# A fused attention, MoE and routed-expert kernel: expert 0's rows gathered before the last tile is stored, and a routing round in fewer instructions

## The chip, the cores and the metric

One core of a Trainium2 chip. The metric is the device time of one execution in microseconds (us), the median of several runs.

Engine names: PE or TensorE does matmuls, PEld is its load of stationary weights, DVE is VectorE, ACT is ScalarE, POOL is GpSimd (it also issues the indirect DMAs), SP is SyncE, which here only issues DMAs.

## What is computed

Three steps, cut to what matters here:

```python
# 1. retention-style attention: x is 3072 tokens x 512
# 2. a dense block
h = x @ w_in;  g = h * np.tanh(softplus(h));  x2 = g @ w_out          # 512 -> 2048 -> 512
# 3. a routed block: 8 experts, each takes exactly 3072 / 8 = 384 tokens
flat = (x2 @ w_gate).flatten()
for idx in np.argsort(-flat):                 # best (token, expert) pairs first
    tok, e = idx // 8, idx % 8
    if assigned[tok] < 0 and counts[e] < 384:
        assigned[tok] = e;  counts[e] += 1
for e in range(8):
    out[assigned == e] = relu(x2[assigned == e] @ w1[e]) @ w2[e]
```

Matrix products are done on pairs of 16-bit halves, three matmuls for one product.

## The kernel before

**Stages.** Tokens go in 8 groups of 384 (`G`), each of 3 tiles of 128 (`C`). For each group the attention, then `h_phase` (the first half of the dense block) and `x_phase` (the second half, a tile at a time: 48 matmuls of 512 columns into one PSUM bank, a square on ScalarE for the scale, a split into two 16-bit halves `xr`, and a DMA of these rows to `xbuf` in DRAM). When the logits of all groups are there, the routing starts while the last seven tiles of `x_phase` still run: three of group 6, three of group 7, and one tile of group 5 that was kept back ("late", its columns reloaded from `gbuf`). Then come the experts 0 to 7, one after the other.

**Routing** (`route_round`, lines 691 to 792) has eight rounds. A round finds which expert fills up next and which tokens it takes: each token's best logit `M` becomes an integer key, its five digits are compared one after the other with all thresholds (`against`, line 686, on VectorE), 24 matmuls count the tokens above each threshold (`pc`, line 729), one matmul spreads the answer (`pn`, line 734), and VectorE goes on to the next digit. At the end two matmuls (`pp`, lines 776 and 777) give each token its place in the expert's list, and the taken tokens' logits in `L` are set to a very low number. `route_list` (line 796) then turns places into a list of row numbers, `IDX[r]`, by 24 matmuls `pl` (line 819).

**An expert's data.** `weights(i)` (line 847; i is 0 for w1, 1 for w2) loads an expert's matrix into a half of `RAW` by an indirect DMA from GpSimd's queue (line 862), squares it on ScalarE in four parts (line 868), and splits it in four parts into `WIN` (even experts) or `WOUT` (odd ones), ScalarE and VectorE each doing one half (lines 228 and 229). `prep_x(r)` (line 885) gathers the expert's 384 rows from `xbuf` by three indirect DMAs (line 890) and turns them: for expert 0 by 24 transposes on TensorE (line 902) and three copies out of PSUM on VectorE (line 903), for the others by a DMA that transposes. `expert(r)` (line 907) has a first half of 8 times 12 matmuls, evicted by lines 918 to 920, and a second half of 3 times 24, evicted by line 936 and scattered to the output by line 937.

**What sets the order.** `Weave` (line 43) is a planner: a main generator yields the cost of what it has just issued, side generators yield a wait after which they are due, and when the planner's clock passes a due time that side issues its next piece. The numbers in `KN` are such waits (`rw`: before a round's counts, `rs`: a correction for each step of each round, `lw`: before a list's matmuls, `fw` and `fs`: the weights' waits). From line 1124 on the instructions of TensorE, and from line 1145 on those of ScalarE, stay in the order in which they were issued; on VectorE, GpSimd and SyncE the order is left to the scheduler of the framework, by priority and readiness. The end of the program, from line 1140:

```python
    wv.add(logits(NG - 1), KN['st'][0]);  wv.add(routing(), KN['st'][1])
    wv.add(lists(), 21.0, 0);  wv.add(weights(0), KN['st'][2], 0);  wv.add(weights(1), KN['st'][3], 0)
    wv.run(x_phase(NG - 2))
    ...
    wv.run(x_phase(NG - 1))
    wv.run(x_phase(NG - 3, late, GB[0]))
    XD.append(1)
    wv.add(tokens())                       # calls prep_x(r) as soon as IDX[r] is known
    for r in range(E):
        need(lambda: r in XTE and r in SPL)
        wv.run(expert(r))
```

Of the kernel before, what the change touches and what calls it, by code (L numbers as in the profile page):

```python
# [39 lines left out]
KN = dict(ea=1, sc=1, pw=4, le=0.0, hl=['P', 'P'], cs=['V', 'V', 'V', 'V', 'V', 'V', 'V'], cc=['V', 'V', 'V', 'V', 'V', 'V', 'V', 'V', 'V'], lo=['c0', 'g', 'c1', 'm', 'c2', 's', 'wg', 'w0', 'w1', 'w2'], ga=['', 'V'], rs=[[-0.63, 0.3, -1.2, 0.0, 0.24, 0.0, 0.09, 0.0, 0.21, 0.0, 0.0, -4.24], [2.1, 0.09, 2.19, 0.0, 0.58, 0.15, 0.18, 0.15, 0.26, 0.26, 1.46, -0.41], [3.26, 0.0, -0.68, 0.2, 0.33, 0.0, -0.3, 0.0, 0.09, -0.12, 0.3, -3.18], [0.56, 0.0, 0.38, 0.0, 0.15, 0.0, 0.12, -0.11, -0.04, -0.27, 0.03, -3.34], [0.67, 0.0, 0.31, -0.76, 0.89, 0.0, 0.15, -0.22, 0.0, 0.0, -0.16, -4.15], [1.46, -2.35, 0.04, -0.29, 0.13, -2.18, 0.42, -0.4, 0.45, 0.03, 1.16, -4.07], [0.45, 0.54, 0.45, 0.0, 1.18, 0.0, -0.39, -0.55, -0.61, -0.05, 0.45, -3.57], [-0.15, 0.0, -0.75, 0.0, 0.0, 0.0, 0.0, -0.3, 0.0, 0.0, 3.28, -3.01]], fs=[[0.0, 0.0, -3.96, -1.22], [-0.75, 0.0, 1.32, 0.16], [0.0, 0.0, -2.08, 0.13], [0.0, -1.13, 0.71, 0.36], [0.0, 0.0, 0.0, -0.56], [0.38, 0.75, 0.13, 0.04], [0.0, 0.38, 0.2, 0.69], [0.0, -1.5, -0.61, 0.29]], av=[5.75, 5.75, 2.0, 4.0], a2=[1.3, 2.2, 4.3], a1=[0.1, 1.0, 0.85], ao=[3.5, 3.5, 3.35], wv=[8.5, 0.5, 1.0, 4.5], ov=5.0, an=[3.0, 3.15, 3.6], qm=['P0', 'VP', 'VP', 'PH', 'P1', 'VV', 'VP'], vm=['P0', 'VP', 'VP', 'VP', 'VP', 'P0', 'VP'], km=['A', 'H', 0, 0, 0, 0, 0], am=['AP', 'AP', 'AP', 'AV', 'AP', 'AV', 'VP'], ss=['V', 'P', 'P', 'P', 'P', 'P', 'P'], sm=['P', 'V', 'V', 'P', 'E', 'D', 'P'], ym=[0, 0, 0], hm=['VVVP', 'VVAV', 'VVVP', 'VVVP', 'AVVP', 'VVVP', 'VVVP', 'VVVP', 'VVVP'], ci=['AP'] * 8, co=['AP'] * 8, wa=[15, 12, 8, -1, 7, 16], cp=[0, 100, 0, 100], np=0, yp=[0, 2000], op=[0, 0, 200, 0, 50, 1000], xp=[0, 0, 0, 0, 0, 0], ld=[0, 1, 2, 3, 4], wj=[4, 4, 4], fw=[13.5, 18.5, 14, 16, 14, 16], qs=1.0, tw=3.0, sw=1.5, po=[[0] * 8] * 4, sl=[0, 0, 0.7], rw=[4.9, 2.5, 1.55, 1.7, 1.7], pn=0.5, lw=14.0, gx=9.0, tk=2.75, st=[16.0, 21.0, 20.0, 23.5], wi=['H', 'A', 0, 0, 2, 0, 0, 0], wo=['H', 'H', 0, 0, 0, 0, 'H', 0], tp=[], gw=5.15, nw=1.0, cw=0, sp=50, ap=1000, wp=None, ip=None)  # L40
# [58 lines left out]
def moe_kernel(ctx, tc, qkv, w_in, w_out, w_gate, w1p, w2p,  # L99
# [32 lines left out]
    V.tensor_scalar(identf, jp, 0.0, None, op0=OP.is_equal)  # L132
    tri = cst.tile([128, 128], BF, name="tri")
    V.tensor_scalar(tri, jp, 0.0, None, op0=OP.is_gt)
# [471 lines left out]
    def x_phase(g, cs=range(CPG), gb=None):  # L606
# [3 lines left out]
        for c in cs:  # L610
# [11 lines left out]
            SY.dma_start(xbuf[r:r + C, :], xr)  # L622
            yield PC[0] * 0.216


    RT, IDX, EWI, EWF = {}, {}, {}, []

    def route_setup():
# [62 lines left out]
    def route_round(r):  # L691
# [150 lines left out]
    def ps_any():  # L842
        return next(banks)()
# [370 lines left out]
```

## Time and profile before

| | us |
|---|---|
| median of 3 runs | 1097.4 (1096.71 to 1100.52) |
| the profiled execution | 1102.12 |
| span of the profile, first to last instruction | 1100.2 |
| TensorE busy | 965.7 |
| VectorE busy | 766.8 |
| ScalarE busy | 664.3 |
| GpSimd busy | 404.3 |

The profile is one execution, 4.7 us above the median. Times inside it are counted from the first instruction. A "view" is an answer that the trace gives: waits by engine, a chain of work followed back from the end, a list of instructions in order of time, or a table by stretch. In a row of the timeline `[1.14 <-DVE se0a L192]` says that the engine sat idle for 1.14 us and that VectorE's line 192 ended that. A row with `x12` is a run of 12 instructions merged; the busy time of a run of matmuls includes the drain of the last one.

### The profile page before, as it was taken

The numbers are of one execution on the slowest core, as the hardware profiler recorded it, in microseconds if no ns is written. First come the engines' busy times: TensorE is split into PE (matmuls) and PEld (weight loads), VectorE is DVE, ScalarE is ACT, GpSimd is POOL, SyncE is SP. The second block draws the span as 40 slices with busy tenths as digits, with TensorE's granted clock in tenths as the row PEclk, the third lists the DMA queues.
The fourth block names the chain that finished last, engine by engine and source line by source line (L and its number), as shares of the span: only waits on it lengthen the run. The fifth ranks groups of instructions, "written<-read, shape, count | busy, mean of one in ns | idle before, by whom it ended". The sixth has DMA issues, their size and how long they took to land.

```text
span 1100.2 us, 19751 instructions
## 1 busy us (share of the span) xinstructions
PE 965.7 (88%) x7897; PEld 558.3 (51%) x7897; DVE 766.8 (70%) x1742; ACT 664.3 (60%) x1010; POOL 404.3 (37%) x289
## 2 busy tenths in 40 slices
PE   3358768878999999999999989999599998989997
PEld 2345544444665555655556546545355554545553
DVE  6799979752666777677786755567778896795430
ACT  6457887742467577577567667415357676567741
POOL 4745553650542653543555423300312402304111
PEclk9959988878999999999999999999699999999999
DMA  9551361148113113122134110032555644728400
GB/s 316 173 156 42 106 192 38 39 91 167 27 53 86 41 49 87 39 64 62 49 87 83 45 39 1 10 117 114 159 177 164 179 148 153 233 84 263 140 29 29
DMA packets 108812, 113.65 MB, mean 103 GB/s; under 512 B 92464, under 2 KB 92592, under 8 KB 106672
## 3 DMA queue, kind: packets, MB, share of 16 engines
q1 hardware_dynamic: 102576, 66.24, 23.5%
q0 software_dynamic: 6144, 46.15, 12.0%
q8 instruction: 62, 1.02, 0.4%
q14 instruction: 30, 0.25, 0.1%
HBM read 77.50 MB, written 13.64 MB: 83 GB/s over the span
## 4 chain that ended last, share of the span: by engine, by line
PE 46%; DVE 23%; issue 12%; ACT 5%; DMA 4%; POOL 4%; SPq 0%; another core or an unknown queue 0%; POOLq 0%; ACTq 0%; DVEq 0%
PE ph L525 18%; PE px L525 18%; DVE ld L686 2%; DVE WIN L229 2%; DVE WOUT L229 2%; DMA yh<-WOUT 1%; DVE RAW L571 1%; DVE ld L373 1%; PE py L434 1%; POOL out_dram L937 1%; DVE G L574 1%; DVE RAW L555 1%; DMA ld<-in_qkv_dram 1%; DVE G L920 1%; DMA G<-x_rows,GQ 1%
## 5 line engine op out<-in xcount | busy, mean ns | idle before, releaser
L525 PE MATMUL ph<-xt,WIN 128*128 128x384 f16 x1728 | 330.8, 334 | 14.2 <-DVE RAW L555 6.3
L525 PE MATMUL px<-WOUT,G 128*128 128x512 f16 x1248 | 312.9, 386 | 2.1 <-DVE WOUT L229 1.5
L525 PEld LDWEIGHTS <-WIN 128*128 128x128 f16 x1920 | 187.4, 101 | 155.6 <-issue 31.7
L525 PEld LDWEIGHTS <-G 128*128 128x128 f16 x1728 | 165.7, 99 | 185.9 <-issue 18.6
L577 POOL TENSOR_TENSOR G<-RAW,G 128x1536 f16<-128x1536 f32 (+1 forms) x32 | 102.0, 3186 | 98.1 <-DVE G L574 78.5
L555 DVE TENSOR_SCALAR RAW<-ph 128x384 f32<-128x384 f32 x124 | 68.2, 551 | 44.2 <-PE ph L525 43.7
L406 POOL TENSOR_TENSOR amt<-amt 128x512 f16<-128x512 f32 x40 | 53.6, 1341 | 122.7 <-DVE amt L403 85.9
L562 ACT ACTIVATE RAW<-RAW,zt,ch 128x1536 f32<-128x1536 f32 x32 | 53.3, 1666 | 43.8 <-DVE RAW L555 40.3
L325 ACT ACTIVATE junk<-ld 128x512 bf16<-128x512 f32 x63 | 39.6, 628 | 62.5 <-DMA ld<-in_qkv_dram 61.4
L868 ACT ACTIVATE junk<-RAW 128x1024 bf16<-128x1024 f32 x64 | 67.5, 1055 | 6.2 <-DMA RAW<-in_w1p_dram,MASK 5.5
L571 DVE TENSOR_TENSOR RAW<-RAW 128x1536 f32<-128x1536 f32 (+1 forms) x33 | 56.5, 1712 | 13.8 <-ACT RAW L570 13.7
L223 POOL TENSOR_TENSOR RAW<-ld,RAW 128x512 f16<-128x512 f32 x34 | 46.5, 1384 | 43.5 <-ACT RAW L222 41.8
L862 POOL DMA_INDIRECT RAW<-in_w1p_dram,MASK x8 | 8.0, 1000 | 144.0 <-ACT G L919 45.9
L228 ACT ACTIVATE WOUT<-RAW,se 128x1024 f16<-128x1024 f32 x32 | 36.0, 1148 | 35.3 <-DVE se L195 35.3
L920 DVE TENSOR_TENSOR G<-G,G 128x384 f16<-128x384 f32 x64 | 35.5, 554 | 31.3 <-ACT G L919 31.1
L400 DVE TENSOR_TENSOR amt<-pa,MASK 128x512 f32<-128x512 f32 x38 | 26.1, 687 | 37.7 <-PE pa L399 30.4
L525 PEld LDWEIGHTS <-WOUT 128*128 128x128 f16 x384 | 36.9, 99 | 24.1 <-issue 0.7
L937 POOL DMA_INDIRECT out_dram<-G,MASK x18 | 25.7, 1426 | 62.5 <-ACT G L936 57.3
L570 ACT ACTIVATE RAW<-RAW 128x1536 f32<-128x1536 f32 (+1 forms) x33 | 47.7, 1445 | 0.4
L563 ACT ACTIVATE RAW<-RAW 128x1536 f32<-128x1536 f32 x32 | 47.2, 1476 | 0.4
L525 PE MATMUL px<-WIN,G 128*128 128x512 f16 x192 | 45.3, 388 | 1.3 <-DVE G L920 0.8
L223 POOL TENSOR_TENSOR STH<-SC,STH 64x256 f16<-64x256 f32 x34 | 29.6, 871 | 45.1 <-ACT STH L222 42.2
(580 smaller groups left out, 1997.7 us busy)
## 6 DMA issues: line engine op xcount, KB each, us to landing
ld<-in_qkv_dram SPq DMA_DIRECT2D x20, 768.0 KB, 4.9
G<-in_w_in_dram SPq DMA_DIRECT2D x8, 1024.0 KB, 7.2
G<-in_w_out_dram SPq DMA_DIRECT2D x8, 1024.0 KB, 5.1
x_rows<-xr SPq DMA_DIRECT2D x24, 256.5 KB, 2.9
G<-in_qkv_dram SPq DMA_DIRECT2D x2, 768.0 KB, 6.6
g_columns<-G SPq DMA_DIRECT2D x1, 1024.0 KB, 8.4
G<-g_columns SPq DMA_DIRECT2D x1, 1024.0 KB, 7.4
ld<-in_qkv_dram SPq DMA_DIRECT2D x3, 256.0 KB
```

The lines of the kernel that those rows point to most:

```text
L223: (V if pool in ("V", "E") else P).tensor_tensor(lo, src, hi, op=OP.subtract)
L229: V.scalar_tensor_tensor(lo, src, s, hi, op0=OP.mult, op1=OP.subtract)
L406: (P if mode[1] == "P" else V).tensor_tensor(amh[:, j, 1], am, amh[:, j, 0], op=OP.subtract)
L525: T.matmul(p, a, b, start=i == 0, stop=i == n - 1)
L555: V.tensor_scalar(hs[:, f], p[:, :G], 1.0 / 65536.0, None, op0=OP.mult)
L562: A.activation(th, hs, AF.Tanh, scale=ch[:, q:q + 1], bias=z)
L563: A.activation(th, th, AF.Arctan, scale=-0.5, bias=0.5)
L570: A.activation(th[:, w], th[:, w], AF.Sin, scale=-2.0, bias=math.pi / 2)
L571: (V if hm[1] == 'V' else P).tensor_tensor(th[:, w], th[:, w], hs[:, w], op=OP.mult)
L577: (P if lo == 'P' else V).tensor_tensor(gb[:, 1, o], th[:, w], gb[:, 0, o], op=OP.subtract)
L868: A.activation(junk(1024), RAW[:, o:o + 1024], AF.Square, accum_out=ss[:, j:j + 1])
L920: V.tensor_tensor(hid[:, 1, f], hs, hid[:, 0, f], op=OP.subtract)
```

## The change

**Expert 0's rows.** The order of the last seven tiles becomes: group 6, the first two tiles of group 7, the late tile of group 5, then the last tile of group 7. Zeroes are stored in that last tile's rows of `xbuf` beforehand. Between the late tile and the last one, `first_rows` issues the three gathers of expert 0's rows, in which the last tile's rows come as zeroes. `first_x` takes the place of `prep_x(0)`: the gathered rows are multiplied by the identity into six PSUM banks in turn, and onto each the last tile's rows, taken from `xr` in SBUF, are added by a matmul with a selection matrix `FIRST["cols"]` that round 0's list makes; ScalarE and VectorE copy three banks each out. Then the same rows are gathered a second time, into the other three buffers, for the scale column that `expert(0)` reads (through a copy `FIRST["scale"]`).

**Two weight steps put off.** The load of expert 1's first matrix is issued after `first_rows`; the splits of expert 0's second matrix are issued when expert 0's rows are there.

**Routing.** The first digit's compare comes before the operations that make `PP`; the prefix sums take one scan and two matmuls into the same bank instead of a copy, a scan and two additions; the expert's number comes from `m1` instead of from a mask; a list makes `mv` in two operations instead of six and a cast.

**Waits of the planner.** `rw[0]` 4.9 to 2.6, `lw` 14 to 11, a new `g0` for `first_x`, and in `rs` and `fs`: the wait before `pp` (index 10) is 2.5 to 3.5 longer in rounds 3 to 6, the wait before a round's counts (index 0) 1.2 shorter in round 4 and 2.5 shorter in round 5, the wait before a list's matmuls (index 11) 0.8 to 2.0 longer in rounds 2, 3 and 5, and one wait of expert 7's weights 3.5 longer.

```diff
     V.tensor_scalar(tri, jp, 0.0, -1.0, op0=OP.is_le, op1=OP.mult)
...
 def route_round(r):
+            V.tensor_scalar(di[:, 0], key, DIGITS[0][0], None, op0=OP.arith_shift_right)
+            cv = rt("cv", [NT, VR], BF, bufs=2)
+            V.tensor_scalar(cv, di[:, 0, :, None].to_broadcast([128, NT, VR]), 65.0, UNIT[0], op0=OP.add, op1=OP.mult)
+            against(cmpt, cv, OP.is_ge, 0)
+            eq = rt("eq", [NT, E])
+            V.tensor_tensor(eq, L, M[:, :, None].to_broadcast([128, NT, E]), op=OP.is_equal)
+            V.tensor_tensor(eq, eq, we[:, None, :].to_broadcast([128, NT, E]), op=OP.mult)
...
+        inc = rt("inc", [2 * NT], BF)
+        V.tensor_tensor_scan(inc, ABf, ABf, 0.0, op0=OP.add, op1=OP.bypass)
+        if not last:
+            ce = rt("ce", [E])
+            V.tensor_scalar(ce, e1, m1, -BIG, op0=OP.is_equal, op1=OP.mult)
+            V.tensor_tensor(L, L, ce[:, None, :].to_broadcast([128, NT, E]), op=OP.add)
+            V.scalar_tensor_tensor(L, AB[:, 0, :, None].to_broadcast([128, NT, E]), -BIG, L, op0=OP.mult, op1=OP.add)
+            V.tensor_scalar(ei, m1, -128.0, RT["row"][:, 0:1], op0=OP.mult, op1=OP.add)
...
-        T.matmul(pp[:, 0].rearrange("p a t -> p (a t)"), tri, ABf, start=True, stop=True)
-        T.matmul(pp[:, 1].rearrange("p a t -> p (a t)"), onesb, ABf, start=True, stop=True)
-        tot = rt("tots", [2 * NT])
-        V.tensor_copy(tot, pp[:, 1].rearrange("p a t -> p (a t)"))
-        inc = rt("inc", [2 * NT])
-        V.tensor_tensor_scan(inc, tot, tot, 0.0, op0=OP.add, op1=OP.bypass)
-        pos = rt("pos", [2 * NT], bufs=2)
-        V.tensor_tensor(pos, inc, tot, op=OP.subtract)
-        V.tensor_tensor(pos, pos, pp[:, 0].rearrange("p a t -> p (a t)"), op=OP.add)
+        T.matmul(pp, tri, ABf, start=True, stop=False)
+        T.matmul(pp, onesb, inc, start=False, stop=True)
...
 def weights(i):
-            while r not in EWI or (r == 1 and KN['ga'][i] and 0 not in XTE):
+            while r not in EWI or (r == 1 and ((KN['ga'][i] and 0 not in XTE) or "rows" not in FIRST)):
...
-            while (r > 1 and r - 2 not in (H2, OUT)[i]) or (r == 1 and not XD):
+            while (r > 1 and r - 2 not in (H2, OUT)[i]) or (r == 1 and not XD) or (r == 0 and i and 0 not in XTE):
...
+    def first_rows():
+        for c in range(CPG):
+            P.indirect_dma_start(out=XG[c], out_offset=None, in_=xbuf,
+                                 in_offset=bass.IndirectOffsetOnAxis(ap=IDX[0][:, c:c + 1], axis=0))
+        FIRST["rows"] = True
+    def first_x():
...
+        def part(c, a, w, cols, first):
+            if first:
+                pp[c, a] = ps_any().rearrange("p (k t) -> p k t", k=KD)
+            for k in range(KD):
+                o = (a * KD + k) * 128
+                T.matmul(pp[c, a][:, k], w[:, o:o + 128], cols, start=first and k == 0, stop=not first and k == KD - 1)
+            if not first:
+                o = xt[:, a, :, c * C:(c + 1) * C]
+                with tc.high_priority():
+                    if a:
+                        V.tensor_copy(o, pp[c, a])
+                    else:
+                        A.activation(o, pp[c, a], AF.Copy)
+        yield KN['g0'][0], 0.0
+        for c in range(2):
+            for a in range(2):
+                part(c, a, XG[c], identh, True)
+        yield KN['g0'][1], 1.0
+        for c in range(CPG):
+            for a in range(2):
+                if c == 2:
+                    part(c, a, XG[c], identh, True)
+                part(c, a, XR[0], FIRST["cols"][:, c, :], False)
+        for c in range(CPG):
+            P.indirect_dma_start(out=XG[CPG + c], out_offset=None, in_=xbuf,
+                                 in_offset=bass.IndirectOffsetOnAxis(ap=IDX[0][:, c:c + 1], axis=0))
+        yield KN['g0'][2], 1.7
...
+    zr = wk.tile([128, ROW], F16, name="xr", tag="xr", bufs=2)
+    V.memset(zr, 0.0)
+    SY.dma_start(xbuf[N - C:, :], zr)
+    wv.run(x_phase(NG - 1, range(CPG - 1)))
     wv.run(x_phase(NG - 3, late, GB[0]))
+    need(lambda: 0 in IDX)
+    first_rows()
+    wv.run(x_phase(NG - 1, range(CPG - 1, CPG)))
```

## Rows read from the trace of the kernel before

**Rows 1.** The page: the span, and TensorE's busy time with its share.
```profile
span 1100.2 us, 19751 instructions
PE 965.7 (88%) x7897; PEld 558.3 (51%) x7897; DVE 766.8 (70%) x1742; ACT 664.3 (60%) x1010; POOL 404.3 (37%) x289
```
**Rows 2.** TensorE's waits, 775 to 799: line, releaser, us in total, times, longest.
```profile
PE pc2x0x L729 <- DVE ld L686: 7.0, 1, 7.0
PE pc2x2x L729 <- DVE ld L686: 4.5, 1, 4.5
```
**Rows 3.** TensorE's waits from 799 to the end: first and last of 17.
```profile
PE pc6x8x L729 <- DVE ld L686: 2.4, 1, 2.4
...
PE pc5x4x L729 <- DVE ld L686: 0.2, 1, 0.2
```
**Rows 4.** Timeline from the last tile into expert 0: start, length, engine, line, operation.
```profile
770.41 5.34 PE L525 MATMUL px<-WOUT,G 128*128 128x512 f16 x24
775.85 0.60 ACT L616 ACTIVATE junk<-px 128x512 bf16<-128x512 f32 x1 [2.12 <-PE px L525]
778.20 0.75 DVE L229 SCALAR_TENSOR_TENSOR xr<-px,st,xr 128x512 f16<-128x512 f32 x1
782.71 2.03 POOL L890 DMA_INDIRECT G<-x_rows,MASK  x1 [10.99 <-issue]
786.30 0.95 POOL L890 DMA_INDIRECT G<-x_rows,MASK  x1 [0.30 <-issue]
791.07 1.01 PE L902 MATMUL ph<-identh,G 128*128 128x128 f16 x8
794.20 0.68 DVE L903 COPY xt<-ph 128x1024 f16<-128x1024 f16 x1
794.94 3.95 PE L525 MATMUL px<-xt,WIN 128*128 128x384 f16 x12 [1.14 <-DVE se0a L192]
801.48 2.12 PE L525 MATMUL px<-xt,WIN 128*128 128x384 f16 x12
```
**Rows 5.** The chain that ended last: the store of the last tile.
```profile
778.98 2.68 DMA x_rows<-xr
```
**Rows 6.** Stretches: length, then PE, PEld, DVE, ACT, POOL busy (instructions), clock, DMA.
```profile
785.00:790.00 5.00, 0.53 (x20) 0.51 (x20) 2.52 (x6) 0.00 (x0) 1.90 (x2) 0.50 0.59 158
795.00:834.00 39.00, 38.01 (x322) 20.73 (x322) 29.02 (x94) 21.91 (x37) 9.06 (x7) 0.95 0.57 156
834.00:876.00 42.00, 39.06 (x358) 21.82 (x357) 37.20 (x106) 29.46 (x50) 13.38 (x10) 1.00 0.58 175
```
**Rows 7.** Timeline, weights: expert 1's first load, a split of expert 0, the load's first square.
```profile
770.78 0.94 POOL L862 DMA_INDIRECT RAW<-in_w1p_dram,MASK  x1 [32.28 <-ACT xr L228]
...
774.31 1.28 DVE L229 SCALAR_TENSOR_TENSOR WIN<-RAW,se,WIN 128x1024 f16<-128x1024 f32 x1
...
780.00 1.06 ACT L868 ACTIVATE junk<-RAW 128x1024 bf16<-128x1024 f32 x1 [1.83 <-DMA RAW<-in_w1p_dram,MASK]
```
**Rows 8.** Timeline, round 0's start: logits done, first compare, first counts.
```profile
709.16 0.24 DVE L601 SCALAR_TENSOR_TENSOR L<-pm,lgf,lgt 128x24 f32<-128x24 f32 x1
712.37 1.76 DVE L686 TENSOR_TENSOR ld<-MASK,ld 128x3072 bf16<-128x3072 bf16 x1
714.19 0.76 PE L729 MATMUL pc0x0x<-MASK,ld 128*128 128x8 bf16 x24
```
**Rows 9.** Groups by form, 760 to 1000: busy us, mean ns, idle before.
```profile
L810 DVE TENSOR_SCALAR GQ<-GQ,ld 128x24 bf16<-128x24 f32 x21 | 5.6, 271 | 0.0
L729 PE MATMUL pc4x0x<-MASK,ld 128*128 128x8 bf16 x24 | 0.7, 166 | 0.0
```
**Rows 10.** Timeline: VectorE beside two of the gathers, and the slowest gather.
```profile
782.61 1.30 DVE L686 TENSOR_TENSOR amt<-GQ,ld 128x1024 bf16<-128x1024 bf16 x2
787.11 0.21 DVE L927 TENSOR_SCALAR GQ<-G,ie 128x1 f32<-128x1 f32 x1 [2.44 <-DMA G<-x_rows,MASK]
...
947.70 2.89 POOL L890 DMA_INDIRECT G<-x_rows,MASK  x1 [0.30 <-issue]
```

More of the change, by code (lines that the diff above doesn't have):

```diff
@@ L745, in route_round @@
             V.scalar_tensor_tensor(e1, pn, tv, we, op0=OP.is_equal, op1=OP.mult)
-            m1 = rt("m1", [1])
+            m1 = RT["first"][:, r:r + 1]
             V.tensor_reduce(m1, e1, axis=AX.X, op=OP.max)
@@ new lines, in route_round @@
+        V.tensor_tensor_scan(inc, ABf, ABf, 0.0, op0=OP.add, op1=OP.bypass)
[5 more added lines that the diff above has]
+            V.tensor_scalar(ei, m1, -128.0, RT["row"][:, 0:1], op0=OP.mult, op1=OP.add)
+            if r == 1:
+                EWF.append(rt("ewf", [1]))
+                V.tensor_scalar(EWF[0], m1, -128.0, RT["row"][:, 0:1], op0=OP.mult, op1=OP.add)
+        else:
+            m1 = rt("rest", [1])
+            V.tensor_reduce(m1, RT["first"][:, :E - 1], axis=AX.X, op=OP.add)
+            V.tensor_scalar(ei, m1, 128.0, RT["row"][:, 1:2], op0=OP.mult, op1=OP.add)
@@ L883, in weights @@
                 SC[r] = ie
+    def first_rows():
[4 more added lines that the diff above has]
+    def first_x():
+        xt = wk.tile([128, 2, KD, G], F16, name="xt", tag="xt", bufs=2)
+        XTE_[0] = xt
+        pp = {}
+        def part(c, a, w, cols, first):
[9 more added lines that the diff above has]
+                        V.tensor_copy(o, pp[c, a])
+                    else:
+                        A.activation(o, pp[c, a], AF.Copy)
[13 more added lines that the diff above has]
+        yield KN['g0'][2], 1.7
     def prep_x(r):
@@ L887, in prep_x @@
         XTE_[r] = xt
+        if r == 1:
+            FIRST["scale"] = rt("fs", [CPG])
+            for c in range(CPG):
+                V.tensor_copy(FIRST["scale"][:, c:c + 1], XG[CPG + c][:, 2 * DM:2 * DM + 2].bitcast(F32))
         for c in range(CPG):
@@ L891, in prep_x @@
                                  in_offset=bass.IndirectOffsetOnAxis(ap=IDX[r][:, c:c + 1], axis=0))
[L892 to L904 removed]
+            turned(xt, c, xg[:, :2 * DM])
         yield KN['gx'], 0.0
@@ L923, in expert @@
             yield 0.5
+        while r == 0 and "scale" not in FIRST:
+            yield 0.5
         fac = rt("fac", [CPG], bufs=3)
@@ L926, in expert @@
             xg = XG[(r % 2) * CPG + c]
-            V.tensor_scalar(fac[:, c:c + 1], xg[:, 2 * DM:2 * DM + 2].bitcast(F32), SC[r], None, op0=OP.mult)
+            xs = xg[:, 2 * DM:2 * DM + 2].bitcast(F32) if r else FIRST["scale"][:, c:c + 1]
+            V.tensor_scalar(fac[:, c:c + 1], xs, SC[r], None, op0=OP.mult)
         H2.add(r)
@@ L1075, in tokens @@
                 yield 1.0, 0.0
-            yield KN['tk'], 0.0
-            yield from prep_x(r)
+            if r:
+                yield KN['tk'], 0.0
+                yield from prep_x(r)
+            else:
+                yield from first_x()
             XTE[r] = XTE_[r]
```

113 lines of the change are left out of this document (45 added, 68 removed).

## The prediction, made before the changed kernel was run

> **What bounds the kernel now.** I read the page first: TensorE is busy for 88% of a span of 1100.2 us [rows 1], so what can be won is TensorE's idle time, and the rest of the reading is a search for where that idle time lies in the stretch the change touches. Call T the end of the last tile of the softplus block: its 24 last matmuls start at 770.41 and take 5.34, so T is 775.75 [rows 4]. Expert 0's first matmul starts at 794.94 [rows 4]. Between them lie 19.19 us.
>
> What fills them is one chain, step by step [rows 4, 5]. The tile is squared on ScalarE at 775.85, split into two halves until 778.95 (778.20 + 0.75), stored to DRAM from 778.98 to 781.66 [rows 5], gathered back from 782.71 (the third gather is issued at 786.30), turned on TensorE from 791.07, copied out until 794.88 (794.20 + 0.68), and only then does expert 0 begin. TensorE's list of waits for this stretch names routing instead (pc2x0 7.0 us, pc2x2 4.5 us) [rows 2], because round 2's counts stand in the same queue; but those two end at 782.77 and 789.49, and the turning of the rows ends last. The chain, not the routing, sets expert 0's start.
>
> A second cost hangs on the gap. The granted clock is 0.50 in it, with 0.53 us of matmul in 5 us [rows 6], and expert 0's first 12 matmuls take 3.95 us where 12 of the same shape take 2.12 later [rows 4]: 1.8 us more. The gap with its tail is 19.2 + 1.8 = 21.0 us.
>
> After it TensorE is nearly always at work: 38.01 of 39 us in expert 0's stretch, 39.06 of 42 in expert 1's [rows 6]. From 799 to the end it waits 17 times, from 2.4 down to 0.2 us, 15.4 us together, the most part for VectorE in the routing [rows 3].
>
> **The change part by part.** Times are against the profiled execution, 1102.12 us (span 1100.2 and 1.9 around it); the median of the runs is 1097.4, 4.7 lower. I apply the difference in us to the median.
>
> *Early gather.* Expert 0's rows of 23 tiles are gathered while the last tile is computed, and the last tile's share is added by 24 matmuls from the tile in SBUF. Store, three gathers and landing leave the path after T. Are the gathers in time? The tile before the last must be stored first. A tile is 48 matmuls, 24 take 5.34, so that tile ends at about T - 11; split and store cost what they cost at T (781.66 - 775.75 = 5.9), so the gathers can be issued from about T - 4 [rows 4, 5]. The three take from 782.71 to 787.25 to issue now, the landing is seen by the turning at 791.07 at the latest, so 4.5 to 8.4 us: done between T + 0.5 and T + 4.4. The last tile's halves are ready at T + 3.2 as now. So the gathers are hidden or late by 1 us.
>
> Then 32 short matmuls follow on the path (24 for the last tile, 8 for the third block of rows; 16 for the first two blocks come sooner). Now 8 of that shape take 1.01 us at the low clock with the drain of the last [rows 4], some 0.11 each: 32 x 0.11 = 3.5 us, half of it at the full clock. The copies out are twice as many halves, shared by ScalarE and VectorE; the last costs about what the copy at 794.20 does, 0.7. T + 3.2 + 3.5 + 0.7 = T + 7.4, and a group of round 2's counts (0.7, rows 9) in between makes it T + 8.1. Bounds: T + 6 (full clock, nothing between) and T + 10 (late gather, two such groups). The clock's tail I take as 1.3 of the 1.8, bounds 0 and 2.
>
> *What the gap hid.* pc2x0, pc2x2 and the list of round 1, 24 matmuls each, cost TensorE nothing in the gap. They now go elsewhere: 3 x 0.7 [rows 9] and 0.2 for small ones, 2.3 us.
>
> *Round 0 starts its counts earlier.* The order of TensorE is written by the planner, and the first wait of a round falls from 4.9 to 2.6 of its units. On the grid of four matmuls this puts pc0x0 two groups earlier, 8 x 0.22 = 1.7 us: at about 712.4 in place of 714.19 (0.22 is 5.34 / 24) [rows 4, 8]. VectorE's chain there runs from 709.40 (709.16 + 0.24) to 714.13 (712.37 + 1.76) and is not much shorter after the change, since the four operations on 128x192 that are moved behind the first compare still have to be done before pc0x0 (it reads both). I count 0.5 us less, so TensorE waits 1.2 to 1.7: 1.4, bounds 0 and 2. In later rounds the chain after the prefix counts loses five operations as well, about what the planner takes off; nothing there.
>
> *Two weight steps put off.* Expert 1's first weight load is emitted after the early gathers, and the four splits of expert 0's second weights after its rows are there. The load is issued at 770.78 now [rows 7]; nobody but expert 1 needs it, some 40 us later, so by itself nothing. The splits are four of 1.28 us on VectorE [rows 7] and as many on ScalarE; they leave the last tile and enter expert 0, with the list and the counts of the gap. VectorE is busy 29.02 of 39 us there now; 29.0 + 5.1 for the splits and some 6 of routing, less 3, is 37, about expert 1's 37.20 of 42 [rows 6]. TensorE idles 2.9 us in expert 1's stretch and 1.0 in expert 0's, so I charge the crowding 2.0, bounds 0 and 4. Behind the splits on GpSimd stands the second weight load of expert 1, which reuses their source; it has expert 0's second half to land.
>
> *Shorter routing.* A round loses about ten short operations and gains three, a list loses seven and gains two or three. At 0.27 for a short one [rows 9] that is at most 3.4 us of VectorE a round. VectorE is not the bound; only the 15.4 us after the gap [rows 3] can shrink. The waits for the prefix counts (pp) are among the easy ones, and the new waits of the planner move those steps 2.5 to 3.5 later. I take -3.0, bounds -6 and +3 (the order is new, so other steps can be early).
>
> *What else moves.* The tile that was last, a tile of group 5, now goes two tiles earlier, so its reload has some 22 us instead of 44 after the tiles of group 6; a store of zeroes goes onto SyncE's queue before the tiles of group 7, where nothing waits long. Neither is on the path. Three more gathers (for the scale column) follow the last store on GpSimd. Expert 1's gathers stand behind them and behind a copy of the scales; they are needed 40 us after T, nothing.
>
> *A rule against it.* The gather issued at 782.71 took 2.03 us, with VectorE at its 16-bit compares, the one at 786.30 took 0.95 while VectorE sat idle until 787.11, and one took 2.89 [rows 4, 10]. The Trainium skill ("SBUF — State Buffer", section "SBUF: two separate sides") says that GpSimd cannot write its DMA descriptors while VectorE holds the port pair that the two share. By that rule the early gathers, which now run beside a busy VectorE, would be slow ones; its price is in the second rival. The trace shows slow and quick ones side by side, so it speaks neither way for certain.
>
> *Sum:* -21.0 + 8.1 + 1.3 + 2.3 + 1.4 + 2.0 - 3.0 = -8.9 us: 1102.1 to 1093.2 on the profiled execution, 1097.4 - 8.9 = 1088.5 on the median.
>
> **The rivals.** *ScalarE is held by the weight squares (no change).* ScalarE's order is written out too. By the planner's numbers the squares of expert 1's first weights come due 13 to 14 units after the load is emitted, at about T + 3.5, and the copies of expert 0's rows at about T + 4.5: one or two squares stand ahead of the copies. The load takes 9.2 us to its first square now (770.78 to 780.00) [rows 7]. If GpSimd issues it behind the gathers, at about T + 0.5, ScalarE waits until T + 9.7, does two squares (1.06 and the read of the sum, 1.2 each) and three copies (2.1): T + 14. That is 5.9 more: -3.0, 1094.4. Against it: the load is ready before the gathers are, and the code writes out the order of TensorE and ScalarE alone, so on GpSimd the load may well go first. *The same, with slow gathers (slower).* If the three gathers take 2.9 each [rows 10] and 0.3 between, the load behind them goes out at T + 6; first square T + 15.2, two squares and three copies T + 19.7, with all four squares ahead T + 22. With the clock low throughout: -21.0 + 22 + 2 + 2.3 + 1.4 + 2 = +8.7, 1106; with two squares ahead 1103.8. It decides as soon as load and gathers are both late. *The experts are not held by their start (no change).* If the rounds set the pace, expert 0 starts earlier and a later expert waits as much longer: 1097. Against it: TensorE is busy 97% and 93% in the first two experts' stretches [rows 6].
>
> **How the numbers follow.** Forecast and its bounds 0.68; ScalarE held 0.14, rounds set the pace 0.06; slow gathers with the load behind, or crowding beyond its bound, 0.12. With every favourable bound (-21.0 + 6 + 2.3 - 5) the forecast reaches 1080; upwards the range takes in the held ScalarE and ends at 1098. About 0.5%, 5.5 us, is what a measurement of this kernel can tell from no change: faster 0.68, same 0.20, slower 0.12.
>
> **What would show it.** From the last px matmul of the tiles to expert 0's first matmul 6 to 10 us; the six copies of expert 0's rows right behind their matmuls, on ScalarE no square between; pc0x0 with a wait of 1 to 2 us for a compare; TensorE's waits after expert 0's start 10 to 16 us in all. A gap of 13 or more with ScalarE waiting for the weight load is the first rival; gathers of 2 to 3 us each with it the second; waits of 10 us or more at a later expert's first matmuls the third. The forecast is wrong if TensorE's waits after the gap grow by more than 6 us.

## The result and the profile after

The changed kernel takes 1112.62 us (median of 4 runs, 1111.74 to 1113.46); the kernel before, run beside it, 1097.99 (1096.71 to 1100.52). The ratio is 1.0136, 95% interval 1.0113 to 1.0158: slower by 15 us where I had forecast 9 us faster. The profiled execution has a span of 1110.6 us, against 1100.2 [rows 1].

```profile
span 1110.6 us, 19699 instructions
PE 972.2 (88%) x7921; PEld 561.6 (51%) x7921; DVE 753.9 (68%) x1627; ACT 665.9 (60%) x1013; POOL 402.2 (36%) x295
```

Line numbers of after are its own: L745 is `pc` (L729 before), L750 `pn`, L791 `pp`, L830 `pl`, L697 `against`, L229 and L230 the splits, L873 the weight loads, L879 their squares, L900 the early gathers.

VectorE has 115 instructions and 12.9 us less, as the diff says, and the kernel is slower all the same. Where the time went is found by cutting the span at expert 0's first matmul. First the timeline of the stretch ahead of it in the changed kernel (start, length, engine, line, operation), to be set against [rows 4]:

```profile
775.20 1.02 PE L526 MATMUL px<-WOUT,G 128*128 128x512 f16 x4
776.03 0.95 POOL L900 DMA_INDIRECT G<-x_rows,MASK  x1 [9.60 <-PE pc2x0x L745]
777.28 2.39 POOL L900 DMA_INDIRECT G<-x_rows,MASK  x1 [0.30 <-issue]
779.54 1.05 ACT L879 ACTIVATE junk<-RAW 128x1024 bf16<-128x1024 f32 x1
779.98 0.94 POOL L900 DMA_INDIRECT G<-x_rows,MASK  x1 [0.30 <-PE px L915]
784.18 0.60 ACT L922 ACTIVATE xt<-ph 128x512 f16<-128x512 f32 x1 [3.51 <-PE ph L915]
787.00 0.48 PE L526 MATMUL ph<-xt,WIN 128*128 128x384 f16 x1
787.91 1.95 PE L526 MATMUL ph<-xt,WIN 128*128 128x384 f16 x11 [0.43 <-DVE xt L920]
```

The last tile ends at T = 776.22 (775.20 + 1.02), expert 0 begins at 787.00: a gap of 10.8 us where there were 19.2. The first twelve matmuls take 2.86 (787.00 to 787.91 + 1.95) in place of 3.95. So the early gather did most of what it was to do. The loss is all behind that point. The two stretches from expert 0's first matmul to the end, before and then after (length, then busy time and instructions of PE, PEld, DVE, ACT, POOL, then the granted clock):

```profile
794.94:1100.20 305.26, 281.36 (x2101) 152.66 (x2100) 198.30 (x574) 183.58 (x312) 69.14 (x55) 0.98 0.48 145
```
```profile
787.00:1110.60 323.60, 287.89 (x2106) 155.11 (x2103) 194.64 (x500) 191.23 (x322) 71.51 (x61) 0.95 0.45 141
```

323.60 against 305.26: 18.3 us more, with less work on VectorE. TensorE is busy 6.5 us longer with nearly the same matmuls (2106 and 2101 in the records), at a mean granted clock of 0.95 instead of 0.98 (summed over slices of 4 us, some 25 us at the lower of its two levels, 1.2 GHz, against some 11), and idle 11.8 us longer (35.7 against 23.9). What it waits for, in the changed kernel from 787 on (line, releaser, us in total, times, longest), answers to [rows 3]:

```profile
PE pc5x0x L745 <- DVE MASK L728: 3.7, 1, 3.7
PE pl3x11x L830 <- DVE GQ L818: 3.3, 1, 3.3
PE pl5x11x L830 <- DVE GQ L818: 2.7, 1, 2.7
PE pc6x0x L745 <- DVE MASK L728: 2.4, 1, 2.4
PE pc4x0x L745 <- DVE ld L697: 1.8, 1, 1.8
PE pc3x0x L745 <- DVE MASK L728: 1.8, 1, 1.8
```

27 waits, 27.3 us; before there were 18 of 16.5 us from expert 0's start on. All the large ones are at the start of a round (`pc` with digit 0) or at a list's matmuls (`pl`), and VectorE ends them. VectorE's own timeline ahead of the largest, in round 5:

```profile
889.62 1.27 DVE L230 SCALAR_TENSOR_TENSOR WOUT<-RAW,se,WOUT 128x1024 f16<-128x1024 f32 x1
890.82 0.15 DVE L763 TENSOR_REDUCE ld<-MASK 128x1 f32<-128x8 f32 x1
890.89 1.27 DVE L230 SCALAR_TENSOR_TENSOR WIN<-RAW,se,WIN 128x1024 f16<-128x1024 f32 x1
...
894.51 0.20 DVE L794 SCALAR_TENSOR_TENSOR MASK<-pp4x10x,MASK 128x48 f32<-128x48 f32 x1
894.62 1.27 DVE L230 SCALAR_TENSOR_TENSOR WOUT<-RAW,se,WOUT 128x1024 f16<-128x1024 f32 x1
...
902.31 0.34 DVE L728 TENSOR_TENSOR MASK<-MASK 128x192 bf16<-128x192 f32 x1
```

Between the short operations of the routing's chain stand weight splits of 1.27 us, and the splits are of both matrices, WIN and WOUT in turn. From the reading of round 4's last spread matmul (888.95) to round 5's first counts (902.71) VectorE is not idle for a moment, and 5.15 us of the 13.76 are splits: its row in the table by stretch, first of all instructions, then of the split's line alone:

```profile
888.95:902.71 13.76, 10.05 (x60) 5.46 (x59) 13.76 (x37) 8.10 (x16) 3.05 (x2) 1.00 0.44 152
```
```profile
888.95:902.71 13.76, 5.15 (x5) 1.00 0.44 152
```

A VectorE that is always busy is not the sign by itself. In the kernel of experiment 6, which is the faster one, the same stretch is 12.19 us long (878.40 to 890.59) and VectorE is busy for 12.14 of them; but 3.82 us of these are splits. One split fewer is 1.3 of the 1.6 us between the two.

Why both matrices at once? GpSimd's loads of the weights tell it, in pairs (the second weights of one expert, the first weights of the next), before and then after:

```profile
795.90 0.94 POOL L862 DMA_INDIRECT RAW<-in_w2p_dram,GQ  x1 [1.40 <-DVE se L196]
815.81 0.94 POOL L862 DMA_INDIRECT RAW<-in_w1p_dram,MASK  x1 [18.96 <-ACT G L919]
838.85 0.96 POOL L862 DMA_INDIRECT RAW<-in_w2p_dram,MASK  x1 [3.77 <-DVE se0a L192]
854.11 0.96 POOL L862 DMA_INDIRECT RAW<-in_w1p_dram,MASK  x1 [12.99 <-ACT G L919]
```
```profile
806.27 1.15 POOL L873 DMA_INDIRECT RAW<-in_w2p_dram,MASK  x1 [10.48 <-DVE MASK L761]
814.59 0.94 POOL L873 DMA_INDIRECT RAW<-in_w1p_dram,MASK  x1 [7.18 <-issue]
852.99 1.03 POOL L873 DMA_INDIRECT RAW<-in_w2p_dram,MASK  x1 [17.65 <-ACT G L965]
862.09 1.36 POOL L873 DMA_INDIRECT RAW<-in_w1p_dram,MASK  x1 [0.30 <-issue]
...
943.11 1.49 POOL L873 DMA_INDIRECT RAW<-in_w2p_dram,MASK  x1 [18.47 <-DVE MASK L747]
944.90 0.96 POOL L873 DMA_INDIRECT RAW<-in_w1p_dram,MASK  x1 [0.30 <-issue]
```

Over the six pairs, the second weights' load goes out 20, 15, 19, 22, 21 and 19 us ahead of the next first weights' before; after, 8, 9, 8, 2 and 5, and in the last pair it is 3 behind. The two weight streams run in step. ScalarE's written-out order shows the same without any time (q a weight square, I a split half into WIN, O into WOUT, a dot an output eviction; expert 0's part ends at the first dot):

```
before   qqqqqqIqIqIIIIIIqqqqOOOOqqqq.Oq.OqOqOq.IIIIqqqq.IqI.qIqIq.OOOOqqqqO.OOOqq.qq.IIIIqqqqIII.I
after    qqqqqIqIqIqIqqqIqIIOIOOO.qq.qqqqq.qOOIOIOII.qqqq.qqqq.IIOIOIOO.qqqqqq.qqO.IOIOIOI.qqqqqq.q
```

Four and four apart before; eight mixed after, in every expert. So theory A was: the put-off of expert 0's second weights' splits delays that stream once, its waits in the planner are fixed numbers from step to step, and so it stays late and runs in step with the other. Theory B: the shorter waits of the planner (`rw[0]`, `lw`, `rs`, `fs`) issue counts and lists before VectorE's chain is done, whatever the weights do.

### The profile page after: what moved, and what is told of

The parts are those of the page before. It is cut to its first block, busy times and chain, and to the rows that moved or that the text cites. A ratio compares the mean times of both kernels' runs of the same rounds, so it can differ in the third digit from the quotient of the medians.

```text
span 1110.6 us, 19699 instructions
## 1 busy us (share of the span) xinstructions
PE 972.2 (88%) x7921; PEld 561.6 (51%) x7921; DVE 753.9 (68%) x1627; ACT 665.9 (60%) x1013; POOL 402.2 (36%) x295
## 3 DMA queue, kind: packets, MB, share of 16 engines
q8 instruction: 62, 1.02, 0.4%
## 4 chain that ended last, share of the span: by engine, by line
PE 48%; DVE 22%; DMA 7%; issue 7%; ACT 7%; POOL 3%; SPq 0%; POOLq 0%; ACTq 0%; DVEq 0%
PE px L526 20%; PE ph L526 19%; DVE WOUT L230 2%; DVE WIN L230 2%; DVE G L967 2%; DMA yh<-WOUT 1%; DVE ld L697 1%; PE py L435 1%; DMA ld<-in_qkv_dram 1%; DVE ld L374 1%; DMA RAW<-in_w2p_dram,MASK 1%; DMA RAW<-in_w1p_dram,MASK 1%; DVE RAW L572 1%; ACT junk L879 1%; POOL amt L407 1%
## 5 line engine op out<-in xcount | busy, mean ns | idle before, releaser
L526 PE MATMUL px<-WOUT,G 128*128 128x512 f16 x1344 | 338.2, 389 | 2.0 <-DVE WOUT L230 1.5
L879 ACT ACTIVATE junk<-RAW 128x1024 bf16<-128x1024 f32 x64 | 67.4, 1053 | 20.3 <-DMA RAW<-in_w1p_dram,MASK 12.5
L572 DVE TENSOR_TENSOR RAW<-RAW 128x1536 f32<-128x1536 f32 (+1 forms) x33 | 56.5, 1713 | 13.9 <-ACT RAW L571 13.7
L526 PEld LDWEIGHTS <-WOUT 128*128 128x128 f16 x384 | 37.0, 99 | 23.9 <-issue 0.4
L987 POOL DMA_INDIRECT out_dram<-G,MASK x18 | 19.8, 1099 | 77.9 <-ACT G L986 73.6
L617 ACT ACTIVATE junk<-px 128x512 bf16<-128x512 f32 x24 | 14.0, 584 | 56.1 <-PE px L526 31.7
L526 PE MATMUL ph<-WIN,G 128*128 128x512 f16 x192 | 46.3, 394 | 0.0
L697 DVE TENSOR_TENSOR ld<-MASK,ld 128x1536 bf16<-128x1536 bf16 (+1 forms) x35 | 44.6, 1275 | 0.5
```

The costliest lines, as they stand in the source:

```text
L526: T.matmul(p, a, b, start=i == 0, stop=i == n - 1)
L572: (V if hm[1] == 'V' else P).tensor_tensor(th[:, w], th[:, w], hs[:, w], op=OP.mult)
L697: V.tensor_tensor(out.rearrange("p t (j v) -> p t j v", v=VR), cv[:, ts, None, :].to_broadcast([128, n, J // VR, VR]), RT["jr"][:, i, :J]. ...
L879: A.activation(junk(1024), RAW[:, o:o + 1024], AF.Square, accum_out=ss[:, j:j + 1])
```

## The experiments

All ratios are to the kernel before, run in the same job (medians 1097.97, 1102.14 and 1097.07 us in the three jobs); intervals are of 95%.

**1. Nothing put off.** The changed kernel less one condition:

```diff
-            while (r > 1 and r - 2 not in (H2, OUT)[i]) or (r == 1 and not XD) or (r == 0 and i and 0 not in XTE):
+            while (r > 1 and r - 2 not in (H2, OUT)[i]) or (r == 1 and not XD):
```

> The changed kernel with one condition taken out: expert 0's second splits are issued as early as before, not when its rows are there. Theory A (the put-off splits delay the second weight stream for good, so that it runs in step with the first and eight splits stand together on VectorE and ScalarE at every round's end): the splits of WIN and WOUT alternate again in groups of four, TensorE's waits after expert 0's start fall from 27 to under 15 us, the time from 1112 to about 1093 (1086 to 1098). Theory B (the planner's shorter waits before counts and lists put these steps earlier than VectorE can be): the waits at pc and pl stay, time 1107 to 1113.

1091.74 us, ratio 0.9938 (0.9917 to 0.9959); one of its eight executions took 1106.15, the others 1087.90 to 1094.43. Waits after expert 0's start 14.7 us. One condition is worth 21 us.

**2. The planner's old waits, splits put off.**

```diff
-rw=[2.6, 2.5, 1.55, 1.7, 1.7], pn=0.5, lw=11.0
+rw=[4.9, 2.5, 1.55, 1.7, 1.7], pn=0.5, lw=14.0
```
and `rs` and `fs` as in the kernel before.

> The changed kernel with the planner's waits of before (rw, lw, rs, fs), the put-off kept. Theory A: the two weight streams still run in step, time 1104 to 1112. Theory B: the waits at the first counts of a round and at the lists go, time about 1092 (1087 to 1097).

1103.12 us, ratio 1.0052 (1.0032 to 1.0072): in neither range, just under theory A's and above theory B's. Its trace shows why it separates nothing. The streams are not in step, as theory A had taken for granted: the old waits move the first weights' loads as well, so that the two loads go out 10 to 15 us apart (878.55 and 889.85, for one) and the splits stand four and four up to expert 5's; only the last pair is close (1004.23 and 1006.35). And the waits at the first counts of rounds 3 to 6 are gone, as theory B had it, but the prefix counts (`pp`) of rounds 4 to 6 now wait 2.1 to 2.3 us each, and a matmul for expert 7's scale waits 4.6 us for a weight square.

**3. Both repairs,** the edits of 1 and 2 together.

> The changed kernel with neither: the planner's waits of before and no put-off of the splits. Both theories: faster than the kernel before, about 1088 (1083 to 1094), since the start of expert 0 keeps its gain of some 7 us. If it is not faster than before, the early gather itself or the shorter routing costs something that neither theory names.

1092.32 us, ratio 0.9949 (0.9934 to 0.9964). With nothing put off the old waits bring nothing that can be measured (0.9949 against 0.9938). The new ones still leave waits of 0.5, 1.9 and 1.7 us at the first counts of rounds 4 to 6 in experiment 1, and here these are gone, without a gain in the time. So theory B is no cause of its own.

**4. The put-off alone,** on the kernel before:

```diff
-            while (r > 1 and r - 2 not in (H2, OUT)[i]) or (r == 1 and not XD):
+            while (r > 1 and r - 2 not in (H2, OUT)[i]) or (r == 1 and not XD) or (r == 0 and i and 0 not in XTE):
```

> The kernel before with the put-off of expert 0's second splits alone. Theory A: the two streams run in step, slower than before by 8 us or more (1106 to 1114). Theory B: no loss beyond expert 0, 1096 to 1101.

1111.86 us, ratio 1.0131 (1.0102 to 1.0159), with nothing gathered early and the old routing: 13.9 us from one condition.

These four leave open whether the put-off costs by the work that it moves into expert 0 or by the phase. Two runs separate that, each changing one number, `fw[3]`, the wait between expert 1's second load and its squares.

**5. The phase alone.** The kernel before, nothing moved:

```diff
-fw=[13.5, 18.5, 14, 16, 14, 16]
+fw=[13.5, 18.5, 14, 26, 14, 16]
```

> The kernel before with a single number changed: the planner's wait between expert 1's second weight load and its squares goes from 16 to 26. No split is put off, nothing is gathered early, the routing is as before. On ScalarE the eight halves of each later expert's weights then stand mixed (first weights, second weights, first, ...) as they do in the changed kernel, instead of four and four. Theory A in its sharp form (what costs is the phase of the two weight streams, not that four splits enter expert 0): 1104 to 1114 us, close to the 1112 of the put-off alone, with TensorE waits of 20 to 25 us after expert 0's start and over 15 us at the low clock. Rival (the moved work itself crowds expert 0's stretch, and the lockstep is only how it looks): nothing is moved, so within 3 us of the kernel before, 1095 to 1101.

1128.04 us, ratio 1.0227 (1.0199 to 1.0254). No work is moved and it is worse than the put-off; larger than I had expected. The second and third pairs of loads are 2 and 1 us apart, the later ones 3 to 4 the other way. Its stretch from expert 0 on, 328.78 us with VectorE busy no longer than before (196.11 against 198.30):

```profile
799.22:1128.00 328.78, 286.02 (x2101) 153.91 (x2100) 196.11 (x574) 184.36 (x312) 59.68 (x55) 0.96 0.48 135
```

**6. Rephased.** The changed kernel, splits still put off:

```diff
-fw=[13.5, 18.5, 14, 16, 14, 16]
+fw=[13.5, 18.5, 14, 8, 14, 16]
```

ScalarE's order from expert 1 on is then `qqqq.O.qOqOqO.qIIIIqqqq.qIq.IqqII.OOOOqqqq`, the same as in experiment 1.

> The changed kernel, the splits still put off, with the same number changed the other way: the wait between expert 1's second weight load and its squares goes from 16 to 8. From expert 1 on, ScalarE's order is then letter for letter that of the kernel without the put-off; in expert 0 the put-off splits stay mixed with expert 1's. Theory A (phase): 1088 to 1097 us, nearly all of the 21 us that leaving out the put-off gave. Rival (moved work): the work is where it was, 1106 to 1113 us. A risk that both share: the load may land later than the eight units, and ScalarE then waits for it once, which would cost a few us.

1094.18 us, ratio 0.9929 (0.9903 to 0.9955): all of the 21 us with the moved work left where it was. Its stretch and its loads, of the same two pairs:

```profile
787.11:1088.30 301.19, 279.86 (x2106) 153.21 (x2103) 197.44 (x500) 191.55 (x322) 68.77 (x60) 0.98 0.52 152
```
```profile
804.65 1.15 POOL L873 DMA_INDIRECT RAW<-in_w2p_dram,MASK  x1 [9.13 <-DVE MASK L761]
812.98 0.94 POOL L873 DMA_INDIRECT RAW<-in_w1p_dram,MASK  x1 [7.18 <-ACT G L966]
836.11 0.99 POOL L873 DMA_INDIRECT RAW<-in_w2p_dram,MASK  x1 [0.30 <-DVE se L196]
848.10 1.01 POOL L873 DMA_INDIRECT RAW<-in_w1p_dram,MASK  x1 [11.00 <-issue]
```

The first pair is 8 us apart as in the changed kernel, for the splits are put off here too; the later ones are 12, 13, 8, 12 and 7 apart, where the changed kernel has 9, 8, 2, 5 and -3. The stretch is 22 us shorter than after's, and VectorE is busy for 2.8 us more than there. The put-off as such is harmless.

**7. The routing alone.** The kernel of experiment 3 with the old end of the program and `prep_x(0)` of before:

```diff
-    wv.run(x_phase(NG - 1, range(CPG - 1)))
+    wv.run(x_phase(NG - 1))
     wv.run(x_phase(NG - 3, late, GB[0]))
-    need(lambda: 0 in IDX)
-    first_rows()
-    wv.run(x_phase(NG - 1, range(CPG - 1, CPG)))
```

> The kernel before with the shorter routing alone: no early gather, no put-off, the planner's waits as before. It splits the gain of the kernel with both repairs (old waits, nothing put off: 1092.3, 5.6 us under the kernel before) into early gather and routing. My prediction held the shorter routing at -3.0 us (bounds -6 and +3) and gap with tail at -8.9 - (-3.0) - 2.0 for the crowding, about -7.9. If that holds: 1094 to 1096. Rival: with the old waits TensorE's order leaves the shorter chain nothing to shorten, so 1097 to 1099, and the whole 5.6 is the early gather's.

1102.62 us, ratio 1.000 (0.998 to 1.002). The rival's case: with the old waits the shorter routing by itself is worth nothing that can be measured. That what the repaired kernels gain is the early gather's follows only by what is left over; the early gather with the old routing was not run.

**8. The scale copies on GpSimd.** Experiment 1 left VectorE idle right behind expert 0's start, in its timeline:

```profile
792.68 0.15 DVE L946 COPY GQ<-G 128x1 f32<-128x1 f32 x1 [4.10 <-DMA G<-x_rows,MASK]
```

The copy of the second gathers' scale stands at the head of VectorE's queue until its gather has landed, and TensorE waits for the counts behind it:

```profile
PE pc2x4x L745 <- DVE ld L697: 4.9, 1, 4.9
```

```diff
-                V.tensor_copy(FIRST["scale"][:, c:c + 1], XG[CPG + c][:, 2 * DM:2 * DM + 2].bitcast(F32))
+                P.tensor_copy(FIRST["scale"][:, c:c + 1], XG[CPG + c][:, 2 * DM:2 * DM + 2].bitcast(F32))
```

> The changed kernel without the put-off, and with the three small copies of the second gathers' scale column on GpSimd instead of VectorE. In the kernel without the put-off VectorE stood idle for 4.1 us at 788.6 to 792.7, because the first of these copies waited for its gather at the head of VectorE's queue, and TensorE then waited 4.9 us for round 2's counts (pc2x4). Theory C (the copies hold VectorE): that wait falls under 1.5 us and the time falls 3 to 5 us under the 1091.7 of that kernel, to 1087 to 1089. Rival (the counts would wait for the chain in front of them anyway, and the stall only hides it): 1090.5 to 1093, with the wait of pc2x4 still over 3 us.

1093.61 us, ratio 0.9917 (0.9892 to 0.9943), against 0.9938 (0.9917 to 0.9959) for experiment 1. The wait went as theory C says:

```profile
PE pc2x4x L745 <- issue: 0.6, 1, 0.6
```

The time did not follow by 3 to 5 us: 2 us, with overlapping intervals, and the waits after expert 0's start add up to 14.9 us, where they were 14.7. pc3x4 is up from 0.3 to 1.7, and a pl4 wait of 1.1 is new. Neither side is shown.

The remaining question is why running in step costs. Theory V: VectorE's row of eight splits delays the routing. Theory L: the two loads share the DMA engines, land late, and hold ScalarE, whose order is fixed. ScalarE's waits for loads from 800 to 1080 in the changed kernel speak for L (in the kernel before there are none, in the rephased one 1.5 us):

```profile
ACT junk L879 <- DMA RAW<-in_w1p_dram,MASK: 10.5, 5, 6.1
ACT junk L879 <- DMA RAW<-in_w2p_dram,MASK: 5.4, 2, 3.1
```

**9. Short splits, streams in step.**

```diff
+            if cols:
+                lo, src, hi = lo[:, :cols], src[:, :cols], hi[:, :cols]
             V.scalar_tensor_tensor(lo, src, s, hi, op0=OP.mult, op1=OP.subtract)
```

with `cols` 128 for the weights of experts 2 to 7.

> The changed kernel as it is (streams in step), but from expert 2 on VectorE's part of each weight split does 128 of its 1024 columns; the rest of the low halves is left out. Order, loads and ScalarE's part stay. It asks why the lockstep costs. Theory V (eight splits in a row, some 10 us of VectorE, stand ahead of the routing's short operations): with the bunch cut to some 2 us TensorE's waits after expert 0's start fall from 27 to 15 us or less, and the time to 1092 to 1099. Theory L (two loads issued together land late, and ScalarE, held by their squares in its fixed order, lets go of its evictions late): nothing of that is touched, so 1107 to 1113. A third kernel of this job gives what the same omission is worth without the lockstep.

1087.84 us, ratio 0.9917 (0.9899 to 0.9935). Order and loads are as in the changed kernel (1.8 us apart at 920), and the waits after expert 0's start fall from 27.3 to 11.1 us.

**10. Loads of experts 2 to 7 left out,** all else as in the changed kernel:

```diff
+            if r < 2:
-            P.indirect_dma_start(out=RAW[:, i * 4096:(i + 1) * 4096], out_offset=None, in_=src,
+                P.indirect_dma_start(out=RAW[:, i * 4096:(i + 1) * 4096], out_offset=None, in_=src,
```

> The changed kernel with the weight loads of experts 2 to 7 left out (squares and splits work on the weights that are there). ScalarE can't be held by a load after expert 1 then; VectorE's work and every order written out stay. Theory L (ScalarE held by loads that land late, 15.9 us of waits in the changed kernel from 800 on, against 1.5 in the rephased one): 1094 to 1102, with TensorE's waits down by half. Theory V (VectorE's bunch): 1108 to 1113.

1107.54 us, ratio 1.0092 (1.0074 to 1.011). ScalarE waits for no load, and TensorE's list is headed by the same rows to the digit:

```profile
PE pc5x0x L745 <- DVE MASK L728: 3.7, 1, 3.7
PE pl3x11x L830 <- DVE GQ L818: 3.3, 1, 3.3
```

Theory L gets some 5 us at most, and 25.0 us of waits stay.

**11. Short splits, rephased:** the edits of 6 and 9 together, the control for 9.

> The rephased kernel (second weight load's wait 8, splits put off) with the same shortened VectorE splits from expert 2 on: the control. 50 us of VectorE are gone (six experts, eight splits of some 1.05 us saved). Under both theories VectorE is not what bounds this kernel, so little: 1088 to 1094, 0 to 6 us under the 1094.2 of the rephased kernel. If it falls by as much as the lockstep kernel with short splits does, that one's fall says nothing for theory V.

1088.11 us, ratio 0.9908 (0.9881 to 0.9934). The same omission is worth some 2 us here (0.9929 to 0.9908, not clear of none) and 24 us in step (1.0136 to 0.9917), and with it the kernel in step and the rephased one are equal. What the lockstep costs is VectorE's time for the splits where they fall there, beside the routing's chain. The kernel before has as many splits of the same length; they stand four and four. That the harm is in a row of eight is not shown: in VectorE's own timeline the rephased kernel's eight follow each other closely too (826.2 to 843.9 and 865.2 to 885.5, against 837.7 to 858.9 and 881.6 to 898.7 in the changed kernel), four of one matrix and then four of the other. Whether the mixing costs, or the steps of the routing beside which the splits fall, no run separates.

**12. Three waits tuned,** on the kernel of experiment 8:

```diff
-rs[2][10] = 0.3;  rs[5][0] = -1.04;  rs[6][0] = 0.45
+rs[2][10] = 2.7;  rs[5][0] = 0.86;  rs[6][0] = 2.15
```

> The changed kernel without the put-off, the scale copies on GpSimd, and three of the planner's waits lengthened by what TensorE waited there: before pp of round 2 by 2.4, before the first counts of rounds 5 and 6 by 1.9 and 1.7. If these waits are simply too short, 3 to 6 us come off the 1093.6 of the kernel with the copies on GpSimd (0.9917 of the kernel before), 0.987 to 0.989. Rival (a wait taken away here comes back at the next step, since the whole round moves with it): 0.990 to 0.994.

No verdict: four executions from 1089.86 to 1114.16, median 1105.95. In the profiled one ScalarE is held by the second weights' load again,

```profile
ACT junk L879 <- DMA RAW<-in_w2p_dram,MASK: 13.7, 2, 9.0
```

and the second weights' loads from 871.92 on go out 15, 18 and 22 us ahead of the next first weights', where experiment 8 has 13, 8 and 12. So taking away a wait where TensorE shows it moved the weights' phase too, but apart and not together. The load issued at 871.92 landed 20.4 us later, where the median of three in experiment 8 is 9.3. It is not the gain that I had looked for; what held that load and what made the spread is open.

Experiments 1, 3, 6 and 8 beat both kernels, by 0.5 to 0.8% against the one before; their intervals overlap, so none is the best.

## Why the prediction was wrong

**Wrong: "Two weight steps put off", 2.0 us, bounds 0 to 4.** It measured 13.9 us by itself (experiment 4) and 21 in the changed kernel (experiment 1). I asked what four splits do to expert 0's stretch, where they land, and put them against VectorE's busy time there. That part was harmless (experiment 6). I put what comes after them in the same stream at nothing: expert 1's second load reuses the source of these splits, so it went out at 806.27 instead of 795.90, and every later step of that stream is due a fixed wait behind the one before. I had written that this load "has expert 0's second half to land", which asks whether it is late for its user, and not what it will then run beside. The rows that could have told it were in the trace of before: the second load is 20 us ahead of the next first load there (795.90 and 815.81), and the put-off took away more than half of that. That the lag stays is seen in the loads; that the planner's fixed waits keep it is read from the code, and only the two changes of one such wait (experiments 5 and 6) support it.

**Wrong in size: "Shorter routing", -3.0.** Experiment 7 has 0 (-2 to +2 us), inside my bounds of -6 and +3. The 12.9 us of VectorE that the profile lost were not what TensorE waited for. What I had said of later rounds, "nothing there", failed with it: the first counts of rounds 3 to 6 wait 1.8, 1.8, 3.7 and 2.4 us in the changed kernel. With nothing put off (experiment 1) they wait 0, 0.5, 1.9 and 1.7, so part of it is the splits' and part is there without them; but with the old waits, which take these away, the time is the same (experiment 3).

**Wrong in place: the gathers "issued from about T - 4".** They went out from T - 0.2 (776.03), and TensorE waited 4.6 us for them where I had 1. What failed here is the store ahead of them, which I let cost what it costs at T, and expert 1's first weight load, which I put at "by itself nothing". That load stands behind the gathers in the program, but GpSimd let it go first, at 765.49, as I had thought possible in the first rival; the store was issued 2.6 us behind it, at 768.08, and landed 6.9 us later, at 774.99. From issue to landing, in the changed kernel and then in experiment 2, where the store goes out ahead of the load (768.81 and 770.68):

```profile
x_rows<-xr SPq DMA_DIRECT2D x1, 256.5 KB, 6.9
RAW<-in_w1p_dram,MASK POOLq DMA_INDIRECT x1, 9.3
```
```profile
x_rows<-xr SPq DMA_DIRECT2D x1, 256.5 KB, 2.6
RAW<-in_w1p_dram,MASK POOLq DMA_INDIRECT x1, 8.7
```

Wherever the store is issued 2.6 us behind the load it takes 6.6 to 7.2 us (experiments 3, 9, 10 and 11 too), and 3.2 and 3.1 where it is issued 6.7 us behind (experiments 1 and 12). The first gather starts 1.0 us after the store's landing in all of these, whatever the profile names as its releaser (pc2x0 here). In experiment 2 it starts at 772.42, 3.7 us ahead of that run's T of 776.09, as I had it, and the gap there is 8.9 us. So the gap is 10.8 instead of 8.1, the clock's tail 0.7 (2.86 - 2.12 [rows 4]) instead of 1.3: gap and tail give -9.5 us, not -11.6.

**Right: the start of round 0** (pc0x0 waits 0.9 us, predicted 1.4; a wait of 0.8 at pc0x2 came with it) **and the first rival's denial:** ScalarE was not held. One square stands ahead of the copies, at 779.54, and its load was there; the copies follow their matmuls by less than a microsecond. Of the second rival's slow gathers one of three came: 0.95, 2.39 and 0.94.

**The rest of the sum held in total.** Without the two terms above it was -21.0 + 8.1 + 1.3 + 2.3 + 1.4 = -7.9 us; with the gap, the tail and round 0's two waits as measured it is -9.5 + 2.3 + 1.7 = -5.5 (no run measures the 2.3 by itself). With the lockstep out, the kernel is 5.6 (experiment 3), 6.8 (1), 7.8 (6) and 9.1 us (8) under the kernel before. That is also inside 1080 to 1098; the range was too narrow only because none of its cases held a lasting shift of one stream against another. My test, "TensorE's waits after the gap grow by more than 6 us", was met: 16.5 to 27.3.

**The third rival, "the rounds set the pace",** had the sign of what happened behind expert 0 (later experts wait as much longer) but not its cause: with the streams apart, the earlier start is kept to the end.

## What to carry to other kernels

When a step of a periodic stream is put off, ask not only whether its user can wait but what the whole stream will then run beside in every later period: if the due times are fixed waits, one delay is a phase shift for good. Two streams that share an engine with a latency-bound chain are worth keeping apart, and the sign to look for in a trace is their loads drawing together, or their splits mixing, from one period to the next. Here loads 15 to 22 us apart (the kernel before) and 7 to 13 (experiment 6) went with splits four and four, and 9 falling to -3 with mixed ones; the ranges touch, so the order of the splits tells it and the distance of the loads alone does not. Test it by changing the phase with no work moved, and by moving it back with the work left where it is; here one number did each.

## What the runs showed of the hardware that I had not expected

Taking some 40 us of work off VectorE was worth 2 us in one order and 24 us in another (experiments 11 and 9: 197.44 to 157.04 us busy from expert 0 on, and 194.64 to 155.85). VectorE's share there had been 66% in the first and 60% in the second: the order in which the cut paid was the one with the lower share.

A gather waits for a 16-bit compare of VectorE that began before it. In the changed kernel the gather of 2.39 us starts at 777.28, 0.17 us behind this one,

```profile
777.11 1.75 DVE L697 TENSOR_TENSOR ld<-MASK,ld 128x3072 bf16<-128x3072 bf16 x1
```

and ends at 779.67, 0.81 us after it. In seven more runs (experiments 1, 2 and 8 to 12) a gather starts beside such a compare with at least half a microsecond of it left, and ends 0.81 to 0.85 us after it, so that it takes 1.41 to 2.60 us by how much was left. A gather that starts 0.1 to 0.4 us ahead of one takes 0.95 to 0.98 (experiments 6, 8, 10 and 12), as in experiment 10:

```profile
780.37 0.95 POOL L901 DMA_INDIRECT G<-x_rows,MASK  x1 [0.30 <-PE pl1x11x L830]
780.47 1.75 DVE L697 TENSOR_TENSOR ld<-MASK,ld 128x3072 bf16<-128x3072 bf16 x1
```

The Trainium skill ("SBUF — State Buffer", section "SBUF: two separate sides") says that of a VectorE operation with two inputs in SBUF and a GpSimd operation that reads SBUF, whichever starts first has the port pair that the two share for its whole instruction, and the other blocks. The order seen here agrees with it for the gathers, 2.39 us behind the compare and 0.95 ahead of it; the compare that starts second is not seen to be held, for it takes 1.75 us in experiment 10 as elsewhere. The same section of the Trainium skill says that a test did not see an operation of this kind (`tensor_tensor`) stall a DMA; in these rows GpSimd is held in issuing one.

A store of 256 KB, which landed in 2.6 us when it was issued ahead of a weight load, took 6.9 when it was issued 2.6 us behind one (experiment 2 and the changed kernel).
